# Attention, experts and a dense layer in one kernel: moving a remainder, a conversion, a subtraction, a clear and two loads

## The chip, the cores and the metric

The kernel runs on one core of one Trainium2 chip. The metric is the device time of one execution in microseconds (us). A core has a matrix engine (TensorE; PE in the profile, with PEld for its weight loads), VectorE (DVE), ScalarE (ACT), GpSimd (POOL), and a queue that issues transfers (SP). Each engine runs its own instructions in their order and waits on the others by semaphores.

## The reference

```
# attention: B=2, H=8, S=576, D=64, with a bias from a small MLP on log distances
scores = q @ k.T / 8 + bias[h, i, j]
attn   = softmax(scores);  x = attn @ v            # (2, 8, 576, 64) -> (1152, 512)

# experts: E=8, F=1024; each token goes to the expert of its highest logit
logits = x @ w_gate;  e = argmax;  g = softmax(logits)[e]
h = relu(x_e @ w1[e]);  y = h @ w2[e]              # up to 288 tokens for each expert
x = g * y  (0 for a token beyond the capacity)

# dense layer: 512 -> 2048 -> 512
h = x @ w_in;  h = max(h, 0) + alpha * min(h, 0);  out = h @ w_out
```

All data is float32; w_in and w_out come as float64 words, which the kernel turns into float32 itself.

## The kernel before

**Attention and routing** (the function course). The work is cut into units (batch, pair of heads, block of 128 queries; a unit of the last 64 queries is called small). For each unit: scores on TensorE, the bias added and the row's minimum taken on VectorE (low), the exponential on ScalarE (expo), transposes of the result (turn), products with v (values). A small unit's last 64 columns are duplicated by GpSimd into a tile named dup, which the transposes read. The bias tables are computed, stored to memory and loaded again by SP. LD[s] lists what SP issues at slot s: load_bias, load (q, k, v), load_vd (a rearranged piece of v), c1 (constants of the routing), clear (zeros written to the rows that the experts read and to the output, from a tile zr that GpSimd fills once). From slot 18 on, the routing of batch 0 runs in small steps between the units, by the list late: one entry a step, two steps a unit. first_weights finds the first expert that has tokens (four small VectorE operations) and lets SP load its first quarter of weights; first_halves, on GpSimd, splits that quarter into a high part and a remainder.

**Experts.** A product in float32 is made as three products of rounded parts: high x high, high x remainder, remainder x high. A quarter q of an expert's weights becomes w1h, w1l, w2h, w2l: the high part by a cast (ScalarE, or GpSimd for the very first), the remainder by a subtraction. job runs an expert group of up to 288 tokens in eight pieces f: layer1(f) makes 12 products (g), a relu (hh) on ScalarE and its remainder (hl) on VectorE; layer2(f-1) makes 12 more (acc). yh and yl are the group's result (to_dense).

The first group's weights are split step by step between the pieces, by the table todo: at key (f, 2) or (f, 4) the words name the steps: hIQ is the cast of w1 (I=1) or w2 (I=2) of quarter Q, lIQ its remainder, so h23 l23 are w2h and w2l of the last quarter, which pieces 6 and 7 use. turn transposes the second group's rows, ahead0 and ahead1 convert pieces 0 and 1 of the last stage's weights from float64 words (f64_convert: a scaling on ScalarE, three VectorE operations, then a cast and a subtraction), jobs3 finishes the list of groups. The order of TensorE, ScalarE and VectorE is that of the code up to the end of this group.

The second group is inside a conditional block (tc.If): the engines take the branch one by one, each when it has done what it has in front of it. Inside, the order on every engine is found by the framework's scheduler. group splits its first quarter with raw_split(0, t, early=True): the cast and the subtraction of w1 on GpSimd. Its steps carry ahead(2), ahead(3), and the rider: a third group of at most 32 tokens whose products run between those of the second, with its weight quarters in borrowed buffers (the last of four in the staging tile M.d[1]).

**The dense layer** (ffn) runs 16 pieces of fg and facc products. Its weights come through three staging tiles M.d, are converted, split, and used; the first four pieces are prepared ahead.

Of the kernel before, what the change touches and what calls it, by code (L numbers as in the profile page):

```python
# [11 lines left out]
F32 = mybir.dt.float32  # L12
# [4 lines left out]
ALU = mybir.AluOpType  # L17
# [5 lines left out]
B, H, S, D = 2, 8, 576, 64  # L23
N, DM = B * S, H * D
# [16 lines left out]
def build(tc, nc, a):  # L41
    V, A, G, T, SY = nc.vector, nc.scalar, nc.gpsimd, nc.tensor, nc.sync
    with contextlib.ExitStack() as ctx:
# [164 lines left out]

        KQV, LAST = {}, [None]

# [418 lines left out]
        def raw_split(q, t, early=False):  # L629

            w = [pair(q, [128, 1024], F32R, n) for n in ("w1h", "w1l", "w2h", "w2l")]
            for i in range(2):
                if early and i == 0:
                    G.tensor_copy(w[0], t[0])
                    G.tensor_tensor(w[1], t[0], w[0].bitcast(F32), ALU.subtract)
                else:
                    halves(w[2 * i], w[2 * i + 1], t[i])
            return w

        def row_tiles():  # L640
            return [raw.tile([128, RW], F32, tag="xr", name="xj", bufs=5)[:96, 0:DM] for _ in range(3)]

        def job_rows(ts, o):
            for r in range(3):
                rows_of.other(SY.dma_start(ts[r], xd[ds(o + 96 * r, 96), 0:DM]))

# [3 lines left out]
        def turn_rows(ts, r, t):  # L650
            for d in range(4):
                T.transpose(t[:, 96 * d:96 * d + 96], ts[r][:, 128 * d:128 * d + 128], ident[:96, :96])

# [93 lines left out]
        def rider(g, e, yo):  # L747
# [9 lines left out]

            def cell2(q):
                S[q] = (AH["more"], *g1.t)[q] if q < 3 else M.d[1].bitcast(F32)
                return S[q]  # L760

            def load1(q):
                SY.dma_start(cell2(q).rearrange("p (k c) -> p k c", k=4),
                             w1[:, 256 * q:256 * q + 256].rearrange("(k p) c -> p k c", p=128))

            def load2(q):
                SY.dma_start(cell2(q).rearrange("p (f n) -> p f n", f=2),
                             w2[256 * q:256 * q + 256, :].rearrange("(f p) n -> p f n", p=128))

# [12 lines left out]
            def partial(q):  # L782
                w = S[q].rearrange("p (k c) -> p k c", k=4)
                ps = ps1(pt, "part")[:, 0:256]
                for k in range(4):
                    T.matmul(ps[n * k:n * k + n], x[:, k], w[:, k], start=True, stop=True, skip_group_check=True)
                R.p = cell()[:, 0:256]
                A.copy(R.p, ps)
# [7 lines left out]
            def layer2(q):  # L796
                if q == 0:
                    R.acc = ps1(pt, "racc")[:, 0:256]
                w = S[q].rearrange("p (f n) -> p f n", f=2)
                for j in range(2):  # L800
                    for d in range(2):
                        o = n * (2 * j + d)
                        T.matmul(R.acc[o:o + n], R.h[:, n * (2 * q + j):][:, 0:n], w[:, j, 256 * d:256 * d + 256],
                                 start=q == 0, stop=q == 3, skip_group_check=True)
# [55 lines left out]
        def fetch_more():  # L860
            z = xp.tile([128, 2048], F32, tag="xT1", name="ah1")
            for j in range(2, PRE):
                AH[j] = z[:, 512 * j - 1024:512 * j - 512]
            AH["more"] = z[:, 1024:2048]
            f64_load(3, M.d[0])
# [123 lines left out]
        def course():  # L989
# [107 lines left out]
            for i in range(n):  # L1097
                u, t, w = [U[z] if z >= 0 else None for z in (i, i - 2, i - 3)]
                s = starts.get(id(u))
                if s is not None:  # L1100
# [138 lines left out]
        def lower(q, i):  # L1239
# [7 lines left out]
        call = dict(st, fetch=fetch_ahead, more=fetch_more, jobs1=jobs1, jobs2=lambda: first(jobs2), jobs3=jobs3,  # L1247
                    turn0=g1.todo[0][1], turn=g1.todo[1][1], **{f"ahead{i}": lambda i=i: ahead(i) for i in range(2)})
        call.update((f"{z}{i + 1}{q}", lambda q=q, i=i, f=f: f(q, i)) for q in range(4) for i in range(2)
# [20 lines left out]
        with tc.If(J.mode == 1) as course:  # L1270
            two_groups(prepare(2, 0), *[(2 * i + 1, lambda i=i: ahead(i)) for i in range(2, PRE)])
            ffn(0, 608)
        with course.Else():
            with tc.If(J.mode > 0) as course:
                group(g1, False, stepper(*[(2 * i + 1, lambda i=i: ahead(i)) for i in range(2, PRE)]))
                ffn(0, 608)
            with course.Else():
                jobs_rest()
                for i in range(2, PRE):
                    ahead(i)  # L1280
# [99 lines left out]
```

## Time and profile before

| | |
|---|---|
| Runs (device us) | 359.82, 360.06, 363.24; median 360.06 |
| The profiled execution | 363.0 us, of which 361.3 us lie between its first and last instruction |
| Granted TensorE clock, mean | 0.992 |
| Busy, share of the span | PE 94%, PEld 76%, DVE 77%, ACT 66%, POOL 17% |
| Transfers | 76.89 MB, mean 213 GB/s |

The busy shares are of the whole span, and the stages have different limits: in the attention part ScalarE and VectorE are nearly as busy as TensorE, in the dense layer TensorE is full. The clock is a share of full speed; it has two levels, 0.5 and 1. In a timeline a line gives the start, the duration, the engine, the line of the code, the operation, what it writes and reads, and in brackets the idle time before it with what ended that. A line may merge several operations (x4). In a view by stretches a line gives the stretch, its length, the busy time (with the number of instructions) of PE, PEld, DVE, ACT and POOL, the granted clock, the share of the transfer engines' time, and GB/s.

### The profile page before, as it was taken

How to read it: one execution, taken by the hardware profiler on the slowest of the kernel's cores; microseconds unless marked ns; L12 is line 12 of the kernel's file. 1: busy time of each engine (PE TensorE's matmuls, PEld its weight loads, DVE VectorE, ACT ScalarE, POOL GpSimd, SP SyncE). 2: the span in 40 equal slices, each digit the busy share in tenths (PEclk: the TensorE clock that was granted, in tenths of full speed). 3: DMA queues.
4: the chain of work that ended last, by engine and by line, in shares of the span. 5: the costliest groups of instructions: out<-in, count | busy, mean ns of one | idle time of the engine just before them, and what ended most of it. 6: DMA issues, size and time to landing. Idle time of an engine off the chain costs nothing. (4 is left out here: it accounts for less than half of the span.)

```text
span 361.3 us, 8966 instructions
## 1 busy us (share of the span) xinstructions
PE 341.3 (94%) x3372; PEld 276.1 (76%) x3373; DVE 278.4 (77%) x673; ACT 237.4 (66%) x585; POOL 61.6 (17%) x91
## 2 busy tenths in 40 slices
PE   4999999998999999999999799999999999999992
PEld 2424565566899888888899797799898898898881
DVE  5979988967788867876788975169999999988330
ACT  6959998986667666767764383348677576566430
POOL 2056333200000010670261400020000000000013
PEclk9999999999999999999999899999999999999998
DMA  7789979897999854928735894653545656430003
GB/s 298 203 261 319 343 262 358 290 306 293 407 352 254 281 190 121 368 97 256 220 96 179 296 319 131 229 175 121 191 156 178 182 166 205 145 118 3 0 14 132
DMA packets 42016, 76.89 MB, mean 213 GB/s; under 512 B 5127, under 2 KB 19591, under 8 KB 41964
## 3 DMA queue, kind: packets, MB, share of 16 engines
q1 hardware_dynamic: 40780, 73.76, 62.2%
q0 software_dynamic: 1184, 2.48, 1.9%
q8 instruction: 28, 0.46, 0.5%
q14 instruction: 24, 0.20, 0.2%
HBM read 57.53 MB, written 20.09 MB: 215 GB/s over the span
## 5 line engine op out<-in xcount | busy, mean ns | idle before, releaser
L273 ACT ACTIVATE p<-p,mn 128x576 f32<-128x576 f32 x72 | 55.6, 779 | 10.7 <-DVE mn L266 10.3
L259 PE MATMUL sps<-kqv 64*128 64x288 f32 x256 | 59.8, 425 | 0.0
L266 DVE CUSTOM_DVE_ANT_0 p<-sps,bias 128x576 f32<-128x576 f32 x72 | 52.2, 750 | 7.4 <-PE sps L252 2.7
L305 PE MATMUL t<-ident,p 64*128 64x64 f32 x640 | 52.5, 227 | 1.9 <-ACT st L200 0.8
L305 PEld LDWEIGHTS t<-ident,p 64*128 64x128 f32 x640 | 45.3, 139 | 6.6 <-ACT st L200 2.5
L183 DVE TENSOR_SCALAR h<-c 128x512 f32<-128x512 f32 (+17 forms) x121 | 49.2, 471 | 0.9 <-PE bps L192 0.8
L280 ACT COPY PT<-t 128x320 f32<-128x320 f32 (+1 forms) x85 | 30.0, 405 | 24.6 <-PE sps L259 18.5
L192 PE MATMUL bps<-h,c 128*32 128x512 f32 (+17 forms) x352 | 36.2, 504 | 6.6 <-DVE h L183 5.1
L259 PEld LDWEIGHTS sps<-kqv 64*128 64x128 f32 x256 | 36.9, 187 | 7.2 <-issue 4.0
L323 PE MATMUL av<-PT,kqv 128*64 128x128 f32 x512 | 35.3, 279 | 0.8 <-ACT pt L280 0.3
L323 PEld LDWEIGHTS av<-PT,kqv 128*64 128x64 f32 x512 | 27.5, 136 | 8.5 <-ACT PT L280 3.7
L845 ACT ACTIVATE cv<-d 128x512 f32<-128x512 f32 x32 | 21.5, 676 | 15.7 <-DMA d<-in_win 7.7
L200 ACT ACTIVATE st<-bps,c 128x527 f32<-128x527 f32 (+35 forms) x72 | 30.8, 507 | 1.0 <-PE bps L192 1.0
L940 PE MATMUL facc<-w2h,hl 128*128 128x512 f32 (+1 forms) x75 | 29.7, 396 | 0.0
L940 PE MATMUL facc<-w2h,hh 128*128 128x512 f32 (+1 forms) x75 | 29.6, 395 | 0.0
L940 PE MATMUL facc<-w2l,hh 128*128 128x512 f32 (+1 forms) x75 | 29.6, 395 | 0.0
L192 PEld LDWEIGHTS bps<-h,c 128*32 128x32 f32 x352 | 11.8, 115 | 23.1 <-DVE h L183 7.3
L179 POOL TENSOR_SCALAR h<-c 128x448 f32<-128x448 f32 (+11 forms) x12 | 21.1, 1761 | 37.0 <-PE bps L192 19.6
L928 PE MATMUL fg<-yh,w1l 128*128 128x304 f32 x120 | 26.6, 302 | 0.0
L928 PE MATMUL fg<-yl,w1h 128*128 128x304 f32 x120 | 26.5, 302 | 0.0
L928 PE MATMUL fg<-yh,w1h 128*128 128x304 f32 x120 | 26.5, 302 | 0.0
L282 DVE COPY PT<-t 128x320 f32<-128x320 f32 (+1 forms) x43 | 18.8, 461 | 8.9 <-PE t L305 8.0
(232 smaller groups left out, 698.2 us busy)
## 6 DMA issues: line engine op xcount, KB each, us to landing
bias<-bd SPq DMA_DIRECT2D x23, 576.0 KB, 6.2
bd<-st SPq DMA_DIRECT2D x36, 295.5 KB, 5.3
raw<-in_ew SPq DMA_DIRECT2D x20, 512.0 KB, 5.5
d<-in_win SPq DMA_DIRECT2D x16, 512.0 KB, 3.8
d<-in_wout SPq DMA_DIRECT2D x16, 512.0 KB, 3.9
kqv<-in_kqva SPq DMA_DIRECT2D x6, 736.0 KB, 6.3
kqv<-in_kqvb SPq DMA_DIRECT2D x6, 672.0 KB, 8.0
xd<-zr SPq DMA_DIRECT2D x4, 722.8 KB, 8.4
```

Of the source, the lines that this page charges most:

```text
L183: V.tensor_scalar(h, tab[:, :n], psi[:, i:i + 1], 0.0, ALU.add, ALU.max)
L192: T.matmul(ps[32 * c:32 * c + 32, n0:n1], w2n, hs[c][:, n0:n1], start=True, stop=True)
L200: A.activation(st[:, o:o + src.shape[1]], src, AF.Copy, scale=rr[:, t:t + 1])
L259: return [lambda n=n: T.matmul(ps[:, n, :288], q[u.ul][p], k[p, 288 * n:288 * n + 288], start=True, stop=True) for n in range(2)]
L266: V.tensor_tensor_reduce(out.rearrange("p (a b) -> p a b", a=2), ps[:, :, :288], bias.rearrange("p (a b) -> p a b", a=2), -0.125, 3.0e38, ...
L273: A.activation(out, out, AF.Exp, bias=mn, scale=-1.0, accum_out=acc)
L280: A.copy(o, i)
L305: return [lambda i=i, x=x: T.transpose(src[:, i], x[p], ident[p, p]) for i, x in enumerate(rows)], out
L323: T.matmul(o[p, c], u.v[:, j, p], rhs(h, j), start=j == 0, stop=False, skip_group_check=True)
L845: A.mul(v, r[:, :, 1].bitcast(F32), 2.0 ** -112)
L928: T.matmul(ps, w[:, 128 * k:128 * k + 128], x[:, k, s], start=k + i == 0, stop=k + i == 5)
L940: T.matmul(acc[i][:m], h[:, r:r + m], w, start=f == 0 and j == 0, stop=f == NF - 1 and j == 2)
```

## The change

Seven things change.

1. h23 l23 move in todo from (6, 2) to (5, 4).
2. ahead1 leaves todo; ahead(1) becomes a step of the second group, in front of ahead(2) and ahead(3) (steps 3, 5 and 7).
3. In raw_split with early, the subtraction that gives the first w1l goes from GpSimd to VectorE.
4. The rider's last weight quarter lies in two of the second group's spare row tiles instead of M.d[1]; each of its two loads becomes two transfers. The row tiles are now declared with all 128 partitions, of which 96 hold rows as before.
5. The two memsets of zr are placed behind the latest dup copy on GpSimd.
6. The loads of vd (batch 1) and c1 go from slots 3 and 4 to slots 7 and 8.
7. In late, first moves two steps later, to the step of s0.

```diff
             if zr is None:
                 zr = raw.tile([128, RW], F32, name="zr")
-                G.memset(zr[:, 0:DM + 1], 0.0)
-                G.memset(zr[:, DM + 1:RW], BIG)
+                behind(G.memset(zr[:, 0:DM + 1], 0.0), DUP[0])
+                behind(G.memset(zr[:, DM + 1:RW], BIG), DUP[0])
...
-                G.tensor_copy(u.dup, u.P[:, 512:576].unsqueeze(1).to_broadcast([128, 2, 64]))
+                DUP[0] = G.tensor_copy(u.dup, u.P[:, 512:576].unsqueeze(1).to_broadcast([128, 2, 64])).ins
...
                 if early and i == 0:
                     G.tensor_copy(w[0], t[0])
-                    G.tensor_tensor(w[1], t[0], w[0].bitcast(F32), ALU.subtract)
+                    V.tensor_tensor(w[1], t[0], w[0].bitcast(F32), ALU.subtract)
...
         def row_tiles():
-            return [raw.tile([128, RW], F32, tag="xr", name="xj", bufs=5)[:96, 0:DM] for _ in range(3)]
+            return [raw.tile([128, RW], F32, tag="xr", name="xj", bufs=5)[:, 0:DM] for _ in range(3)]
...
-            def cell2(q):
-                S[q] = (AH["more"], *g1.t)[q] if q < 3 else M.d[1].bitcast(F32)
-                return S[q]
+            def cells(q, n):
+
+                t = [(AH["more"], *g1.t)[q]] if q < 3 else g.ts[1:]
+                z = [z.rearrange("p (k c) -> p k c", c=n) for z in t]
+                S[q] = [x[:, j] for x in z for j in range(x.shape[1])]
+                return z
+
+            def load(q, w, n):
+                z = cells(q, n)
+                for x, y in zip(z, (w,) if len(z) == 1 else (w[:, 0:512 // n], w[:, 512 // n:])):
+                    SY.dma_start(x, y)
...
-            LD[3].append((lambda: behind(load_vd(1), LAST[0]),))
-            LD[4].append((lambda: behind(SY.dma_start(c1, a["c1"]), LAST[0]),))
+            LD[7].append((lambda: behind(load_vd(1), LAST[0]),))
+            LD[8].append((lambda: behind(SY.dma_start(c1, a["c1"]), LAST[0]),))
...
-                                  "slots first places", "r2", "s0", "r3", "s1", "r4 s2", "s3", "s4 second", "", "halves", ""):
+                                  "slots places", "r2", "first s0", "r3", "s1", "r4 s2", "s3", "s4 second", "", "halves", ""):
...
                 (2, 4): "h12 l12", (3, 2): "jobs2 turn0 h22", (3, 4): "l22", (4, 2): "ahead0 more", (4, 4): "h13 l13 jobs3",
-                (5, 4): "ahead1", (6, 2): "h23 l23", (7, 2): "turn"}
+                (5, 4): "h23 l23", (7, 2): "turn"}
...
-            two_groups(prepare(2, 0), *[(2 * i + 1, lambda i=i: ahead(i)) for i in range(2, PRE)])
+            two_groups(prepare(2, 0), *[(2 * i + 1, lambda i=i: ahead(i)) for i in range(1, PRE)])
```

The other branches of the block change in the same way (range(1, PRE) in place of range(2, PRE)), and the rider's partial and layer2 read the weights through the list S[q].

## Rows read from the trace of the kernel before

**Rows 1.** Stretches of 10 us.
```profile
200.00:210.00 10.00, 7.83 (x51) 7.42 (x51) 7.72 (x11) 4.76 (x10) 3.73 (x2) 0.83 0.85 306
210.00:220.00 10.00, 9.92 (x76) 8.90 (x76) 9.57 (x15) 7.11 (x11) 0.00 (x0) 1.00 0.67 205
220.00:230.00 10.00, 10.00 (x89) 7.45 (x92) 2.15 (x4) 3.11 (x10) 0.00 (x0) 1.00 0.78 249
```

**Rows 2.** Timeline of TensorE at the seam: start, us, what, idle before it.
```profile
202.45 0.55 PE L652 MATMUL xjT<-ident,xj 96*128 96x96 f32 x4 [0.86 <-DVE hl L685]
...
202.78 0.77 PE L696 MATMUL acc<-hh,w2h 128*128 128x288 f32 x4
...
205.39 1.33 PE L696 MATMUL acc<-hh,w2l 128*128 128x288 f32 x4 [1.31 <-DVE w2l L1240]
...
209.04 0.69 PE L681 MATMUL g<-xh,w1h 128*128 128x288 f32 x4
...
209.57 0.70 PE L681 MATMUL g<-xh,w1l 128*128 128x288 f32 x4
```

**Rows 3.** A stretch of 1 us at the seam, columns as in rows 1.
```profile
206.00:207.00 1.00, 1.00 (x7) 1.00 (x5) 1.00 (x3) 0.00 (x0) 0.00 (x0) 0.50 0.12 30
```

**Rows 4.** Timeline of all engines around the seam.
```profile
192.59 0.69 DVE L848 SCALAR_TENSOR_TENSOR cw<-cv,cw 128x512 int32<-128x512 int32 x1
...
197.78 0.45 DVE L685 SCALAR_TENSOR_TENSOR hl<-g,hh 128x288 fp32r<-128x288 f32 x1
...
200.05 0.62 ACT L602 CAST ah<-cw 128x512 fp32r<-128x512 f32 x1 [3.56 <-DVE cw L849]
...
201.56 2.69 POOL L635 TENSOR_TENSOR w1l<-raw,w1h 128x1024 fp32r<-128x1024 f32 x1
...
202.31 3.02 DVE L1240 TENSOR_TENSOR w2l<-raw,w2h 128x1024 fp32r<-128x1024 f32 x1
...
209.91 0.76 DVE L829 TENSOR_TENSOR yl<-acc,yh 128x576 fp32r<-128x576 f32 x1 [0.28 <-ACT yh L828]
...
211.06 1.23 DVE L603 TENSOR_TENSOR w2l<-raw,w2h 128x1024 fp32r<-128x1024 f32 x1 [0.40 <-ACT w2h L602]
...
213.51 1.22 DVE L603 TENSOR_TENSOR w1l<-raw,w1h 128x1024 fp32r<-128x1024 f32 x1
```

**Rows 5.** Timeline of TensorE late in the second group.
```profile
235.99 0.29 PE L696 MATMUL acc<-hh,w2h 128*128 128x288 f32 x1
```

**Rows 6.** Timelines of GpSimd, SP's queue and TensorE before the first group.
```profile
156.12 2.37 POOL L983 TENSOR_TENSOR w1l<-raw,w1h 128x1024 fp32r<-128x1024 f32 x1
...
160.24 0.97 POOL L543 DMA_INDIRECT xd<-xr,ci  x1 [0.46 <-issue]
...
162.64 1.29 SPq L645 DMA_DIRECT2D xj<-xd  x3
...
167.61 0.88 PE L652 MATMUL xjT<-ident,xj 96*128 96x96 f32 x8
```

**Rows 7.** Timeline of all engines around the clear's memsets.
```profile
85.56 0.20 ACT L273 ACTIVATION_READ_ACCUMULATOR p<-p,mn 128x1 f32 x1
...
86.94 0.53 POOL L129 MEMSET zr<- 128x513 f32 x1 [18.60 <-ACT PT L280]
...
87.79 0.27 PE L305 MATMUL t<-ident,dup 64*128 64x64 f32 x2 [1.00 <-POOL dup L276]
```

**Rows 8.** Timelines of VectorE and TensorE around the first weights' choice.
```profile
147.18 0.17 DVE L358 TENSOR_SCALAR f<-ebk 128x8 f32<-128x8 f32 x1
...
148.49 0.48 DVE L282 COPY PT<-t 128x320 f32<-128x320 f32 x1
...
149.02 0.46 PE L305 MATMUL t<-ident,p 64*128 64x64 f32 x7 [0.53 <-DVE PT L282]
```

**Rows 9.** Timelines of SP's queue and of TensorE, first half.
```profile
37.16 0.83 SPq L221 DMA_DIRECT2D vd<-in_vd  x1
...
58.19 0.27 PE L305 MATMUL t<-ident,p 64*128 64x64 f32 x1 [0.81 <-ACT st L200]
```

More of the change, by code (lines that the diff above doesn't have):

```diff
@@ L206, in bias_out @@
             SY.dma_start(dst, st[:, :nr + nf])
-        KQV, LAST = {}, [None]
+        KQV, LAST, DUP = {}, [None], [None]
         def load(b, hp, part="a"):
@@ L640, in row_tiles @@
         def row_tiles():
-            return [raw.tile([128, RW], F32, tag="xr", name="xj", bufs=5)[:96, 0:DM] for _ in range(3)]
+            return [raw.tile([128, RW], F32, tag="xr", name="xj", bufs=5)[:, 0:DM] for _ in range(3)]
         def job_rows(ts, o):
             for r in range(3):
-                rows_of.other(SY.dma_start(ts[r], xd[ds(o + 96 * r, 96), 0:DM]))
+                rows_of.other(SY.dma_start(ts[r][:96], xd[ds(o + 96 * r, 96), 0:DM]))
         def x_tiles(q=0):
@@ L651, in turn_rows @@
             for d in range(4):
-                T.transpose(t[:, 96 * d:96 * d + 96], ts[r][:, 128 * d:128 * d + 128], ident[:96, :96])
+                T.transpose(t[:, 96 * d:96 * d + 96], ts[r][:96, 128 * d:128 * d + 128], ident[:96, :96])
         def split_rows(x, r, t, few=None):
@@ L756, in cell @@
                 return M.p.tile([128, 512], F32, tag="cw", name="cell", bufs=4)
-            def cell2(q):
-                S[q] = (AH["more"], *g1.t)[q] if q < 3 else M.d[1].bitcast(F32)
-                return S[q]
+            def cells(q, n):
[7 more added lines that the diff above has]
+                    SY.dma_start(x, y)
             def load1(q):
-                SY.dma_start(cell2(q).rearrange("p (k c) -> p k c", k=4),
-                             w1[:, 256 * q:256 * q + 256].rearrange("(k p) c -> p k c", p=128))
+                load(q, w1[:, 256 * q:256 * q + 256].rearrange("(k p) c -> p k c", p=128), 256)
             def load2(q):
-                SY.dma_start(cell2(q).rearrange("p (f n) -> p f n", f=2),
-                             w2[256 * q:256 * q + 256, :].rearrange("(f p) n -> p f n", p=128))
+                load(q, w2[256 * q:256 * q + 256, :].rearrange("(f p) n -> p f n", p=128), 512)
             def begin():
@@ L782, in partial @@
             def partial(q):
-                w = S[q].rearrange("p (k c) -> p k c", k=4)
+                w = S[q]
                 ps = ps1(pt, "part")[:, 0:256]
                 for k in range(4):
-                    T.matmul(ps[n * k:n * k + n], x[:, k], w[:, k], start=True, stop=True, skip_group_check=True)
+                    T.matmul(ps[n * k:n * k + n], x[:, k], w[k], start=True, stop=True, skip_group_check=True)
                 R.p = cell()[:, 0:256]
@@ L798, in layer2 @@
                     R.acc = ps1(pt, "racc")[:, 0:256]
-                w = S[q].rearrange("p (f n) -> p f n", f=2)
+                w = S[q]
                 for j in range(2):
@@ L802, in layer2 @@
                         o = n * (2 * j + d)
-                        T.matmul(R.acc[o:o + n], R.h[:, n * (2 * q + j):][:, 0:n], w[:, j, 256 * d:256 * d + 256],
+                        T.matmul(R.acc[o:o + n], R.h[:, n * (2 * q + j):][:, 0:n], w[j][:, 256 * d:256 * d + 256],
                                  start=q == 0, stop=q == 3, skip_group_check=True)
@@ L861, in fetch_more @@
             z = xp.tile([128, 2048], F32, tag="xT1", name="ah1")
-            for j in range(2, PRE):
-                AH[j] = z[:, 512 * j - 1024:512 * j - 512]
-            AH["more"] = z[:, 1024:2048]
+            AH[2], AH[3], AH["more"] = z[:, 0:512], z[:, 512:1024], z[:, 1024:2048]
             f64_load(3, M.d[0])
@@ L1245, in build @@
                 (2, 4): "h12 l12", (3, 2): "jobs2 turn0 h22", (3, 4): "l22", (4, 2): "ahead0 more", (4, 4): "h13 l13 jobs3",
[1 row of a table removed]
+                (5, 4): "h23 l23", (7, 2): "turn"}
         call = dict(st, fetch=fetch_ahead, more=fetch_more, jobs1=jobs1, jobs2=lambda: first(jobs2), jobs3=jobs3,
-                    turn0=g1.todo[0][1], turn=g1.todo[1][1], **{f"ahead{i}": lambda i=i: ahead(i) for i in range(2)})
+                    turn0=g1.todo[0][1], turn=g1.todo[1][1], **{f"ahead{i}": lambda i=i: ahead(i) for i in range(1)})
         call.update((f"{z}{i + 1}{q}", lambda q=q, i=i, f=f: f(q, i)) for q in range(4) for i in range(2)
@@ L1274, in build @@
             with tc.If(J.mode > 0) as course:
-                group(g1, False, stepper(*[(2 * i + 1, lambda i=i: ahead(i)) for i in range(2, PRE)]))
+                group(g1, False, stepper(*[(2 * i + 1, lambda i=i: ahead(i)) for i in range(1, PRE)]))
                 ffn(0, 608)
@@ L1278, in build @@
                 jobs_rest()
-                for i in range(2, PRE):
+                for i in range(1, PRE):
                     ahead(i)
```

## The prediction

> **What bounds the kernel now.** I read the page's busy shares first: TensorE is at work for 94% of the span (the table above), so a gain has to be a wait of TensorE that goes, and any new wait of TensorE is a loss. I then read the trace in stretches of 10 us to find where TensorE is not full. From 30 to 350 us one stretch stands out: 200 to 210 us, where it is busy for 7.83 of 10 us and its granted clock averages 0.83 [rows 1]. That is the seam between the first group of experts and the second. The remaining waits were read off the timeline of TensorE, one by one; those that the change touches come below.
>
> The seam in detail. Three things add up. The last four transposes of the second group's rows wait 0.86 us for an hl, and the twelve products of piece 6 stop for 1.31 us at w2l [rows 2]. Then the clock is at half, 1.2 GHz instead of 2.4 [rows 3]. Four products of 288 columns take 0.53 us undisturbed (209.04 to 209.57 us), so the 24 from 202.78 to 209.04 us should take 3.2 us; they take 6.26, which is 3.1 lost, the 1.31 included. With the 0.86 the seam costs 3.9 us: 2.2 of waiting and 1.7 of slow clock.
>
> Why w2l is late: the remainder l23 is a subtraction on VectorE that takes 3.02 us here [rows 4], where one of the same shape takes 1.22 (213.51 us). GpSimd runs the first w1l of the next group from 201.56 to 204.25 us, almost the same time. Why hl is late: the second converted piece, ahead(1), stands in front of it. ScalarE waits 3.56 us for VectorE's conversion before it can cast, and the relu of piece 6 is behind that cast [rows 4].
>
> The Trainium skill, "GPSIMD Engine Reference", section "1. Specifications", says that GpSimd shares its SBUF interfaces with VectorE and gets in the way of VectorE instructions with two SBUF inputs. The trace agrees, 3.02 against 1.22 us. If that were the only thing that counted, taking the subtraction off GpSimd would bring back the seam's whole 3.9 us; the next part says why I do not take that.
>
> **The change part by part.**
>
> *l23 two slots earlier, ahead(1) out of piece 5.* VectorE is then free after the hl of piece 5 at 198.2 us (197.78 plus 0.45, [rows 4]); l23 takes 1.22 and is done by 199.5, before GpSimd's work starts. The hl of piece 6 follows at about 199.9 instead of just before 202.45 us, in time for the transposes, and nothing that TensorE needs in pieces 6 and 7 is late. The raw buffer that l23 frees is refilled earlier too, which only helps. Gain 3.9 us in the profiled execution; if the clock doesn't fall there in ordinary runs, 2.2.
>
> *First w1l on VectorE.* This is the price. The subtraction is inside the conditional block, and an engine runs its block only after what it has before it. The row that shows this: VectorE's first work in the block, w2l at 211.06 us, comes after the last yl of the group before (209.91 us for 0.76) [rows 4]. So w1l can start at 210.67 us in the old clock, which is 1.63 us after TensorE begins the new group (209.04), and it ends 1.22 later, at 2.85. The second set of four products of that group needs it at 0.53. GpSimd had it at 204.25 us, long before. If TensorE does nothing in between, it waits 2.85 - 0.53 = 2.3 us. The block isn't in a hand-written order, and the trace shows that a product of a step written later is put between two of an earlier one where the earlier one's operand is late: one acc product at 235.99 us, inside a g step [rows 5]. The next piece's eight products with w1h are ready, and they take 2 x 0.53 = 1.06 us. Then the wait is 1.2 us. Bounds: 0 and 2.3 us, and 4.0 if the clock falls as well (the 1.7 from above). I take 1.2, because the block shows such filling.
>
> *ahead(1) in the second group.* Its VectorE work is four operations of at most 0.69 us (one stands in [rows 4]), so up to 2.8 us, plus the w1l of 1.22. In the first 10 us of the group VectorE is already busy for 9.57, in the next 10 for 2.15 [rows 1]. So there is room, but late. What TensorE needs early is the next w1l (213.51 us, [rows 4]). Bounds for its delay beyond TensorE's own: 0, if the added conversions stand behind it, and 1.9 us, if the first w1l (1.22) and one conversion (0.69) stand in front and nothing gives way. I take 0.4, nearer to the lower end, because most of the added work can wait until 220 us and TensorE, held at the first w1l, comes later as well; that wait is the cover.
>
> *The last piece of the rider in the row tiles.* Two transfers in place of one, twice. SP's queue has two more issues of 0.43 us each (three row loads take 1.29, [rows 6]). Behind them in the queue are the loads of the last quarter and of the next stage, none of which TensorE waits for in this group. The staging buffer d1 comes free at ahead(1) instead of after the rider's last product, so the final stage's first load is earlier. No wait of TensorE stands there, so both are worth 0; if the loads are what is late next, the two issues cost 0.9, and -0.9 to 0.9 are the ends that I keep.
>
> *The clear behind the copy.* GpSimd spends 86.94 to 87.5 us on the two memsets and only then makes the copy of the remainder (dup), whose data ScalarE had ready at 85.76 (85.56 plus 0.20). TensorE waits 1.00 us for it [rows 7]. With the memsets behind the later copy, dup is done by about 86.1 and the wait is gone. The memsets feed stores that are issued several steps later, so they cost nothing at their new place. Gain 0.6 (the memsets alone) to 1.0; I take 1.0.
>
> *The first weights' choice two steps later.* Its four small VectorE operations, of 0.17 us like the first, begin at 147.18 us, and the copy of PT behind them and the slot arithmetic starts at 148.49; TensorE waits 0.53 for that [rows 8]. Moved, that wait goes, and the same four are added two steps later, where they may delay a copy in the same way. So the gain is 0 to 0.5; I take 0.4. The load of the first expert's first quarter starts one unit later on SP, some 4 us by my estimate; behind it there stand the row loads, which wait for the scatters anyway.
>
> *Constants later.* vd and c1 leave SP's queue at 37 to 40 us and come back some 20 us later. The stores of the bias tables around them move by up to 0.8 us, the issue time of vd [rows 9]. TensorE's longest wait from 30 to 80 us is 0.81 us, for ScalarE, not for a transfer. So 0, with -0.5 to 0.5.
>
> **The sum.** Against the profiled execution (363.0 us, span 361.3): 3.9 + 1.0 + 0.4 - 1.2 - 0.4 = 3.7 gained, 359.3 us. That execution is 2.9 us longer than the median of 360.06, and its slow clock of 1.7 us may be part of this, since the two quicker runs must save something somewhere. Without it the gain against the median is 2.2 + 1.0 + 0.4 - 1.2 - 0.4 = 2.0, which gives 358.1 us; with it 356.4. I take 358.1 for the median.
>
> **The rivals.**
>
> *A. The wait moves to w1l.* VectorE's w1l stands behind the yl, TensorE has nothing to fill with, and the clock falls there instead. For: 2.3 us is longer than each of the two waits that now lower the clock. Against: the filling in [rows 5]. Price 2.3 + 1.7 + 0.4 against gains of 2.2 + 1.4, so 0.8 slower than the median: 360.9 us. It decides from the point at which the new wait, with its clock, is more than the 3.6 us gained. The Trainium skill, "TensorE: Matmul & The Clock Gate", section "Part 1: The HAM clock gate (the "warmup" mystery)", has it that an engine left idle falls to 1.2 GHz; the trace agrees, 0.50 in [rows 3].
>
> *B. GpSimd's order turns against the scatters.* In the kernel before, GpSimd makes the first w1h and w1l up to 158.5 us, and the last scatter goes out at 160.24; the row loads follow at 162.64, and TensorE takes the rows at 167.61 [rows 6]. If the later load leaves the w1h and w1l in front of the last scatter, this slips by up to 4 us. From the issue of the last row load (162.64 plus 1.29) to their use are 3.7 us, in which they have to land, so the slack is between 0 and 3.7 and the wait between 0.3 and 4; I take 2. Against: GpSimd's order isn't written by hand, and with the load late the scatters are ready first. Time 358.1 + 2 = 360.1.
>
> *C. Everything is covered.* The wait at w1l is filled by other products too (the rider's transposes and partial products), and the clock had fallen in the median run. 360.06 - 3.9 - 1.4 + 0.4 = 355.2 to, without the clock, 356.9; I take 356.
>
> **How the numbers follow.** My forecast has 0.55 (its own range 356.4 to 359.5), A 0.20, B 0.10, C 0.15. The range for 8 in 10 runs from C's time to A's: 355.8 to 360.9. A measurement of this kernel can tell about 1% from no change, 356.5 to 363.7 us. C and the lower edge of the forecast lie below that: faster 0.19. Slower by over 1% needs several of the upper bounds at once, or an order in the block that I don't see: 0.04. The rest, 0.77, is within 1%.
>
> **What would show it.** In the changed profile: l23 near 1.2 us and before 200 us; no wait of TensorE at w2l; the granted clock at 1.00 in the old seam; the dup copy ahead of the zr memsets and no wait behind it; a new wait of TensorE for a w1l of the second group, of 1 to 2.3 us, right after the last yl, and eight products of the next piece in front of it if filled. Wrong would be: no such wait (C), a half clock behind it (A), row transposes that wait near 167 us (B), or VectorE late with the next w1l by more than 1 us.

## The result, and the profile after

The changed kernel takes 363.09 us (median of 20 executions, 360.61 to 366.24) against 360.48 us for the kernel before on the same chip (358.1 to 365.81). The ratio is 1.0074, with a 95% interval of 1.0050 to 1.0098: some 2.7 us slower, less than 1%. The forecast was 358.1 us with a range up to 360.9, so it was wrong by 5 us and in its sign; 0.4 us of this lie in the kernel before, which takes 360.48 us here and 360.06 where the forecast started. The profiled execution is at 365.01 us, its span 363.3, the granted clock 0.989 on average. The profiled executions of two experiments below (e2 and e7) were longer than those kernels' ordinary ones; their rows are read for single waits, not for the total.

The first view is again that of 10 us stretches: length, busy time (instructions) of PE, PEld, DVE, ACT, POOL, granted clock, transfer share, GB/s. These are the lines that answer to [rows 1]:

```profile
200.00:210.00 10.00, 7.82 (x59) 7.59 (x59) 7.41 (x12) 6.32 (x11) 1.04 (x1) 0.94 1.07 360
210.00:220.00 10.00, 10.00 (x73) 9.22 (x71) 8.42 (x13) 5.32 (x10) 0.00 (x0) 0.89 0.45 139
```

The seam was repaired and TensorE is exactly as little busy as before, 7.82 of 10 us against 7.83, and in the next stretch the clock is now below 1. The timelines of TensorE and VectorE say what took the place of the old waits. They answer to [rows 2, 4].

```profile
200.09 1.16 PE L652 MATMUL xjT<-ident,xj 96*128 96x96 f32 x12
...
204.28 0.82 PE L681 MATMUL g<-xh,w1h 128*128 128x288 f32 x5
207.28 0.79 PE L681 MATMUL g<-xh,w1l 128*128 128x288 f32 x4 [2.18 <-DVE w1l L635]
...
208.88 1.16 PE L681 MATMUL g<-xl,w1h 128*128 128x288 f32 x4
...
197.48 1.22 DVE L1244 TENSOR_TENSOR w2l<-raw,w2h 128x1024 fp32r<-128x1024 f32 x1
...
202.09 1.01 DVE L603 TENSOR_TENSOR xl<-xjT,xh 128x384 fp32r<-128x384 f32 x2
204.35 1.55 DVE L835 TENSOR_TENSOR yl<-acc,yh 128x576 fp32r<-128x576 f32 x2 [1.24 <-ACT yh L834]
205.99 1.23 DVE L635 TENSOR_TENSOR w1l<-raw,w1h 128x1024 fp32r<-128x1024 f32 x1
```

Read from the top. The twelve transposes run without a wait, where four of them waited 0.86 us [rows 2]. l23 takes 1.22 us and is over before 199 us, where it took 3.02 [rows 4]. The second group begins at 204.28, 4.19 us after the first transpose; in [rows 2] it began at 209.04. So far every step came as forecast. Then TensorE stops for 2.18 us at w1l. VectorE makes it at 205.99, right behind the last yl, in front of which it stood idle for 1.24 us. Only one product of the next piece fills the gap ("x5" in place of x4), not eight. Four products that take 0.53 us at full clock are 0.96 us apart from 208.88 on, and a stretch of 1 us there shows why:

```profile
210.00:211.00 1.00, 1.00 (x6) 1.00 (x5) 1.00 (x2) 0.03 (x1) 0.00 (x0) 0.50 1.08 333
```

The granted clock is 0.50, the lower of the two levels (1.2 GHz), as it was at the old seam [rows 3]; TensorE had been idle for 2.18 us and back at work for about 1.5 when it fell. By the two rows of 10 us above, the fall costs 1.7 us (10 x 0.06 and 10 x 0.11). That is rival A, place and mechanism.

The early part, which answers to [rows 7, 8]:

```profile
82.94 0.29 POOL L276 COPY dup<-p 128x128 f32<-128x128 f32 x1 [14.80 <-ACT p L273]
91.15 0.29 POOL L276 COPY dup<-p 128x128 f32<-128x128 f32 x1 [7.92 <-ACT p L273]
91.56 0.53 POOL L129 MEMSET zr<- 128x513 f32 x1
...
153.36 1.09 PE L323 MATMUL av<-PT,kqv 128*64 128x128 f32 x16 [1.65 <-issue]
```

The dup copy no longer stands behind the memsets, and no wait of TensorE stands at it. The wait of 0.53 us at 149 us [rows 8] is gone too, but TensorE now loses 1.65 us at 153 us, two steps later, where the choice of the first expert was put. The row names no engine that ended it ("issue"), so its cause isn't shown. In the last stage this execution lost 2.4 us more between 319 and 332 us, after a transfer that came late:

```profile
264.29 0.66 ACT L851 ACTIVATE cv<-d 128x512 f32<-128x512 f32 x1 [2.58 <-DMA d<-in_wout]
...
325.78 0.55 PE L932 MATMUL fg<-yh,w1h 128*128 128x304 f32 x2 [0.59 <-ACT g L935]
```

### The profile page after: what moved, and what is told of

It reads as the page before. It is cut to its first block, busy times and chain, and to the rows that moved or that the text cites. A ratio compares the mean times of both kernels' runs of the same rounds, so it can differ in the third digit from the quotient of the medians.

```text
span 363.3 us, 8967 instructions
## 1 busy us (share of the span) xinstructions
PE 342.3 (94%) x3372; PEld 275.6 (76%) x3373; DVE 277.6 (76%) x674; ACT 236.8 (65%) x585; POOL 60.6 (17%) x90
## 5 line engine op out<-in xcount | busy, mean ns | idle before, releaser
L259 PE MATMUL sps<-kqv 64*128 64x288 f32 x256 | 60.7, 426 | 0.2 <-DVE mn L266 0.2
L192 PE MATMUL bps<-h,c 128*32 128x512 f32 (+17 forms) x352 | 35.2, 503 | 7.5 <-DVE h L183 5.5
L179 POOL TENSOR_SCALAR h<-c 128x448 f32<-128x448 f32 (+11 forms) x12 | 22.4, 1866 | 36.2 <-PE bps L192 18.5
```

Of the source, the lines that this page charges most:

```text
L179: G.tensor_scalar(h, tab[:, :n], psi[:, i:i + 1], 0.0, ALU.add, ALU.max)
L192: T.matmul(ps[32 * c:32 * c + 32, n0:n1], w2n, hs[c][:, n0:n1], start=True, stop=True)
L259: return [lambda n=n: T.matmul(ps[:, n, :288], q[u.ul][p], k[p, 288 * n:288 * n + 288], start=True, stop=True) for n in range(2)]
```

## The experiments

The theories. W: the loss is the first w1l on VectorE, because of its place behind the last yl, with the slow clock behind the wait. R: VectorE has too much to do in the second group, whatever the order. L: the last stage has become slower for a lasting reason. E: an early edit costs. Later, for the seam, V (its old waits vary from one execution to the next) against C (they are always there). S is the prediction's own term for the later choice of the expert. All ratios are to the kernel before on the same chip, with 95% intervals.

**e1: w1l back on GpSimd, all else changed.**

```diff
-                    V.tensor_tensor(w[1], t[0], w[0].bitcast(F32), ALU.subtract)
+                    G.tensor_tensor(w[1], t[0], w[0].bitcast(F32), ALU.subtract)
```

> The changed kernel with one thing undone: the first w1l goes back to GpSimd. Theory W (the wait for w1l on VectorE, 2.2 us, and the half clock behind it, 1.6, are what makes the change slow): both are gone, l23 stays near 1.2 us, the second group starts at about 204 us without a wait, and the time is 1 to 2.5 us under the kernel before, 0.993 to 0.997. Theory L (the last stage is bound by VectorE's chain of conversions, so that what TensorE gains at the seam is given back there as waits for hl and g, and more VectorE work in the second group makes it worse): the wait for w1l goes, but TensorE waits 1 to 4 us in the last stage, and the time is 0.998 to 1.006 of before.

Measured: 357.38 us, ratio 0.9943 (0.9922 to 0.9964), faster than both kernels. GpSimd has the quarter early, and TensorE takes it without a wait:

```profile
199.06 2.40 POOL L635 TENSOR_TENSOR w1l<-raw,w1h 128x1024 fp32r<-128x1024 f32 x1
...
203.19 0.70 PE L681 MATMUL g<-xh,w1l 128*128 128x288 f32 x4
```

The last stage takes 109.48 us from its first product to the start of its last, as in the kernel before, and L had 0.998 or more. One line of the change is worth more than the whole loss.

**e2: the seam alone.** l23, ahead(1) and the rider's last quarter are as changed; w1l is on GpSimd, and the clear, the constants and the first choice are as before.

```diff
-                (5, 4): "ahead1", (6, 2): "h23 l23", (7, 2): "turn"}
+                (5, 4): "h23 l23", (7, 2): "turn"}
```

> The kernel before with only the moves at the seam: l23 two slots earlier, ahead(1) in the second group, the rider's last quarter in row tiles; w1l on GpSimd, the clear, the constants and the first weights' choice as before. Theory W: the seam's 2.2 us of waiting and up to 1.7 of slow clock go, nothing takes their place: 0.991 to 0.996. Theory L: the seam's waits go, the last stage takes back what TensorE gained: 0.998 to 1.005. Theory E (one of the early edits is what costs): like W, since no early edit is in it.

Measured: 359.46 us, ratio 1.0009 (0.9980 to 1.0038). From the first row transpose to the second group it takes 4.19 us, no wait in it, and still nothing is gained, where W had 0.991 to 0.996. That was the second surprise. The time lies in L's range, but the last stage takes its 109.48 us here too, so L's mechanism isn't there. The profile also shows what the clear can cost when it stays where it was:

```profile
88.88 0.53 POOL L129 MEMSET zr<- 128x513 f32 x1 [21.26 <-DMA kqv<-in_kqvb]
...
89.72 0.37 PE L305 MATMUL t<-ident,dup 64*128 64x64 f32 x2 [3.28 <-POOL dup L276]
```

The memsets wait for a load here, and the copy behind them waits too: 3.28 us of TensorE, where [rows 7] had 1.00.

**e3: the early part alone** (clear, constants, first choice; seam and w1l as before).

```diff
-            LD[3].append((lambda: behind(load_vd(1), LAST[0]),))
+            LD[7].append((lambda: behind(load_vd(1), LAST[0]),))
...
-                                  "slots first places", "r2", "s0", "r3", "s1", "r4 s2", "s3", "s4 second", "", "halves", ""):
+                                  "slots places", "r2", "first s0", "r3", "s1", "r4 s2", "s3", "s4 second", "", "halves", ""):
```

> The kernel before with only the three early edits: the clear behind the copy, the constants later, the first weights' choice two steps later. Theory W: the wait of 1.0 us at dup and that of 0.5 at PT go, some of it comes back as a wait near 153 us: 0.996 to 0.999. Theory L: the earlier start of all later stages carries VectorE with it, so the same 0.996 to 0.999. Theory E: a new wait of 1.7 us or more near 153 us, or a later start: 1.002 to 1.007.

Measured: 359.73 us, ratio 0.9986 (0.9957 to 1.0015), 0.5 us against 1.4 in the prediction; E, which had 1.002 or more, falls. Its seam, which is that of the kernel before, waits 0.72 and 1.32 us, but at full clock. These rows are used below:

```profile
198.31 1.04 POOL L634 CAST w1h<-raw 128x1024 fp32r<-128x1024 f32 x1 [9.30 <-DMA raw<-in_ew]
199.44 2.70 POOL L635 TENSOR_TENSOR w1l<-raw,w1h 128x1024 fp32r<-128x1024 f32 x1
...
198.71 1.18 DVE L603 TENSOR_TENSOR ah<-cw,ah 128x512 fp32r<-128x512 f32 x1 [0.69 <-ACT ah L602]
...
200.19 3.03 DVE L1240 TENSOR_TENSOR w2l<-raw,w2h 128x1024 fp32r<-128x1024 f32 x1
```

**e4: w1l on VectorE alone**, in the kernel before.

```diff
-                    G.tensor_tensor(w[1], t[0], w[0].bitcast(F32), ALU.subtract)
+                    V.tensor_tensor(w[1], t[0], w[0].bitcast(F32), ALU.subtract)
```

> The kernel before with only the first w1l on VectorE. l23 isn't slowed by GpSimd any more, so it takes 1.2 us instead of 3.0 and the wait at w2l is gone or under 0.3 us; the wait of 0.86 us for hl at the transposes stays; a wait of 2 to 2.4 us for w1l comes at the start of the second group. Theory W: with the clock at half after it, 1.000 to 1.006. Theory L: the last stage's VectorE chain is 1.2 us longer at its start; 1.002 to 1.008.

Measured: 362.88 us (six executions), ratio 1.0109 (1.0069 to 1.0148), the highest ratio of all and above what either theory had. The wait is there by itself, behind the yl again, and one product stands in front of it again. The clock stays at 1.00 behind it in this profile.

```profile
206.86 0.90 PE L681 MATMUL g<-xh,w1h 128*128 128x288 f32 x5
209.77 0.81 PE L681 MATMUL g<-xh,w1l 128*128 128x288 f32 x4 [2.01 <-DVE w1l L635]
...
206.85 1.55 DVE L829 TENSOR_TENSOR yl<-acc,yh 128x576 fp32r<-128x576 f32 x2
208.49 1.23 DVE L635 TENSOR_TENSOR w1l<-raw,w1h 128x1024 fp32r<-128x1024 f32 x1
```

Together e1 and e4 show which edit loses the time. They don't show why: place (W) or load (R).

**e5: w1l still on VectorE, but in front of the last yl.** GpSimd makes a second cast of the same quarter for it, and w1l lies in the space that ahead(1) fills later.

```diff
+        def w1l_first():
+            t, s = g1.t[0], AH["more"].bitcast(F32R)
+            g1.l = AH["z"][:, 2:4].rearrange("p a b -> p (a b)")
+            G.tensor_copy(s, t)
+            V.tensor_tensor(g1.l, t, s.bitcast(F32), ALU.subtract)
...
-                (5, 4): "h23 l23", (7, 2): "turn"}
+                (5, 4): "h23 l23", (7, 2): "turn w1l_first"}
```

> The changed kernel, but the first w1l of the second group is subtracted on VectorE in the hand-written order behind the row transposes of piece 7, in front of the two last yl (GpSimd makes a second cast of the same quarter for it, and w1l lies in the space of ahead(1)). VectorE still does the subtraction, 1.22 us. W (the cost is the place behind the last yl): VectorE stood idle for 1.24 us in front of that yl, so the subtraction fits there, TensorE's wait of 2.18 us at w1l is gone, the clock stays full behind it, and the time falls by 3.8 to 4.7 us against the changed kernel, to 357 to 358 us, ratio to the kernel before 0.992 to 0.997. R (VectorE has too much to do in the second group, whatever the order): the same work stays in the same 20 us, at most the wait of 2.18 us moves to the next w1l, and the ratio stays at 1.003 or more.

Measured: 358.15 us, ratio 0.9980 (0.9955 to 1.0006), a little short of W's 0.992 to 0.997. On the same chip the changed kernel (e7, below) has 1.0067, so the place is worth 2.8 us (360.98 against 358.15), the added cast included. VectorE does the same subtraction in the gap in front of the yl:

```profile
200.61 1.01 DVE L603 TENSOR_TENSOR xl<-xjT,xh 128x384 fp32r<-128x384 f32 x2
201.54 1.22 DVE L1252 TENSOR_TENSOR ah<-raw,ah 128x1024 fp32r<-128x1024 f32 x1
202.87 1.55 DVE L836 TENSOR_TENSOR yl<-acc,yh 128x576 fp32r<-128x576 f32 x2
...
203.32 0.69 PE L682 MATMUL g<-xh,ah 128*128 128x288 f32 x4
```

The yl starts 0.08 us after the second group, exactly as in e1, and TensorE doesn't wait. R falls: the engine and its load are the same, only the order differs (e10, below, takes load away and keeps the order).

**e6: w1l needed four products later.**

```diff
-                if f == 0:
+                if f == 0 and given:
                     terms = [terms[i] for i in (0, 2, 1)]
```

> The changed kernel, with the terms of the first piece of the second and third group in the order w1h xh, w1h xl, w1l xh, so that w1l is needed after eight products and not after four. W: the wait at w1l is 2.18 less the 0.53 us of four products, 1.65 us; if the clock still falls behind it the time is 0.5 us less than the changed kernel, 362.5; if 1.65 us is too short to bring the clock down, 2 us less, 361. R: no change of the time, 363.

Measured: 360.79 us, ratio 1.0054 (1.0019 to 1.0089). The wait shrinks as W has it, though a little less, and the clock stays at 1.00 behind it. The time is 0.2 us below e7's, less than the intervals can tell, so by the time alone R's "no change" fits as well. In this profile the last stage loses 2.1 us, as in the profile after.

```profile
205.38 0.81 PE L681 MATMUL g<-xh,w1l 128*128 128x288 f32 x4 [1.78 <-DVE w1l L635]
```

**e7: the changed kernel again.** No edit.

> The changed kernel once more, for a second profile. If the wait of 2.18 us at w1l, the half clock behind it and the 2.4 us lost late in the last stage belong to the kernel, all three stand here again and the ratio to the kernel before is 1.0074 as measured. If the half clock and the late loss belong to one execution, only the wait stands here, with the last stage at 109.5 us and the second group at some 38 us.

Measured: 360.98 us, ratio 1.0067 (1.0038 to 1.0097). All three losses stand in this second profile, the wait with the same 2.18 us, 0.50 for the clock at 210 to 212 us, and the late transfer. The clock falls once more, behind waits of 0.89 and 0.27 us at the first group's row transposes:

```profile
207.70 0.79 PE L681 MATMUL g<-xh,w1l 128*128 128x288 f32 x4 [2.18 <-DVE w1l L635]
...
264.78 0.66 ACT L851 ACTIVATE cv<-d 128x512 f32<-128x512 f32 x1 [2.58 <-DMA d<-in_wout]
...
168.00:171.00 3.00, 3.00 (x34) 2.17 (x34) 0.78 (x3) 0.67 (x4) 0.00 (x0) 0.50 0.94 331
```

**e10: ahead(1) back in the first group at (6, 2), w1l still on VectorE.**

```diff
-                (5, 4): "h23 l23", (7, 2): "turn"}
+                (5, 4): "h23 l23", (6, 2): "ahead1", (7, 2): "turn"}
```

> The changed kernel with ahead1 put back into the hand-written order at (6, 2), the first w1l still on VectorE and l23 still at (5, 4). W: the wait at w1l stays between 2.0 and 2.3 us, since it comes from the place behind the last yl, and the time stays at 362 to 364 us. R: without the 2.8 us of ahead(1) in the second group VectorE has room, the second group takes 36 us, and the time falls to 359 to 360 us.

Measured: 361.07 us, ratio 1.0072 (1.0040 to 1.0105), no better than the changed kernel. VectorE comes later to the second group, so part of the wait is now one line earlier, at xl, and the rest at w1l; the seam is 1.05 us longer than the repaired 4.19 and the wait is 1.47, together 2.5 against 2.18. R had 359 to 360.

```profile
204.28 0.89 PE L681 MATMUL g<-xh,w1h 128*128 128x288 f32 x5 [0.64 <-DVE xl L603]
206.64 0.80 PE L681 MATMUL g<-xh,w1l 128*128 128x288 f32 x4 [1.47 <-DVE w1l L635]
```

The filler is one product here too, with a wait of 1.47 as with 2.18 or 2.01 (in e6, with its other order, there is none). The order of TensorE in the built kernel holds just that product at that place, whatever happens in the execution.

**e8: e1 without the later constants and the later choice** (so seam, clear, and w1l on GpSimd; the constants are back at slots 3 and 4).

```diff
-                                  "slots places", "r2", "first s0", "r3", "s1", "r4 s2", "s3", "s4 second", "", "halves", ""):
+                                  "slots first places", "r2", "s0", "r3", "s1", "r4 s2", "s3", "s4 second", "", "halves", ""):
```

> The seam with w1l on GpSimd and the clear, without the later constants and without the later choice of the first expert. W: those two are worth nothing or cost a little (the waits at 150 to 156 us that came with the later choice are 1.1 us in the profile against 0.5 us that went at 148.5), so the time is that of the version with all but w1l, or 0.5 us less: ratio to the kernel before 0.991 to 0.996, and the wait of 0.53 us at 149 us stands again. S (the prediction's own term for the later choice): 0.4 us more than that version.

**e12: e1 again, on the chip of e8.** No edit to e1.

> The changed kernel with w1l back on GpSimd once more, beside its parts on one chip. If the first measurement holds, ratio 0.994; by the version with w1l in front of the yl, which has the same waits in its profile, 0.998. The sum of the parts' profile terms (seam 2.2 to 3.9, clear 0.9, second group and first choice -0.9) says 2.2 us without the half clock, 0.994.

Measured: e8 357.91 us, ratio 0.9956 (0.9928 to 0.9985); e12 358.00 us, 0.9969 (0.9941 to 0.9997). The old wait is back in e8, and it doesn't make it slower:

```profile
148.33 0.46 PE L305 MATMUL t<-ident,p 64*128 64x64 f32 x7 [0.53 <-DVE PT L282]
```

In its place e12 waits further on, at the first group's row transposes:

```profile
165.24 1.13 PE L652 MATMUL xjT<-ident,xj 96*128 96x96 f32 x8 [0.69 <-DMA xj<-xd]
```

So the later choice and constants bring nothing that can be measured. Both versions are faster than both kernels.

**e11: the clear alone**, in the kernel before.

```diff
-                G.memset(zr[:, 0:DM + 1], 0.0)
-                G.memset(zr[:, DM + 1:RW], BIG)
+                behind(G.memset(zr[:, 0:DM + 1], 0.0), DUP[0])
+                behind(G.memset(zr[:, DM + 1:RW], BIG), DUP[0])
```

> The kernel before with the clear's memsets behind the dup copy, and nothing else. W: the wait of 1.00 us at the dup copy is gone, 0.6 to 1.0 us less, ratio 0.997 to 0.9985. Rival: the memsets' delay holds the stores of the clear or the wait moves to another copy, ratio 1.000 or more.

Measured: 358.43 us, ratio 0.9983 (0.9952 to 1.0013): 0.6 us, with zero inside the interval. No wait stands at the dup copy.

**e13: the seam alone again.** No edit to e2.

> The seam part alone with w1l on GpSimd once more, for an undisturbed profile. W: no wait at the seam, some 0.7 us given back in the second group, so 1.5 to 2 us less than the kernel before, ratio 0.994 to 0.996, and a dup wait of 1 us. Rival: the seam's waits were hidden in most executions and the part is worth nothing, as the first measurement said, ratio 1.000.

Measured: 358.74 us, ratio 0.9996 (0.9967 to 1.0025). Nothing again, with a clean seam of 4.19 us. So what it replaces can't usually have cost 2 us.

**e14, e15, e16: the kernel before, three more profiles.** One execution each, beside one of 360.67 us.

> The kernel before once more, for its profile. Theory V (the seam's collision depends on which engine starts its subtraction first, and that varies): in some executions w2l starts before GpSimd's w1l and takes under 1.6 us, and from the row transposes to the second group it is 5.0 us; in others GpSimd is first, w2l takes 3.0 us and it is 6.8 to 8.3 us. Theory C (constant collision): 6.8 to 8.3 us each time, and the seam part must then lose 2 us elsewhere.

> As the run before it: V gives 5.0 us in some of the three, C 6.8 to 8.3 us in all.

> As the two runs before it: V gives 5.0 us in some of the three, C 6.8 to 8.3 us in all.

Measured: 357.58, 358.88 and 360.05 us. From the first transpose to the second group they take 4.98, 4.98 and 5.00 us, against 8.28 in the profile of [rows 2], where the first transpose starts at 200.76 us:

```profile
200.76 0.82 PE L652 MATMUL xjT<-ident,xj 96*128 96x96 f32 x8
```

In all three TensorE waits only at the transposes, 0.23 to 0.25 us, not at w2l, and the clock stays at 1.00. These are rows of e14:

```profile
198.25 0.82 PE L652 MATMUL xjT<-ident,xj 96*128 96x96 f32 x8
...
199.31 0.55 PE L652 MATMUL xjT<-ident,xj 96*128 96x96 f32 x4 [0.23 <-DVE hl L685]
...
203.23 0.77 PE L681 MATMUL g<-xh,w1h 128*128 128x288 f32 x4
...
198.19 0.69 DVE L603 TENSOR_TENSOR ah<-cw,ah 128x512 fp32r<-128x512 f32 x1 [0.69 <-ACT ah L602]
...
199.43 1.43 DVE L1240 TENSOR_TENSOR w2l<-raw,w2h 128x1024 fp32r<-128x1024 f32 x1 [0.18 <-ACT w2h L1237]
...
198.24 1.54 POOL L634 CAST w1h<-raw 128x1024 fp32r<-128x1024 f32 x1 [8.81 <-ACT ah L602]
199.86 3.26 POOL L635 TENSOR_TENSOR w1l<-raw,w1h 128x1024 fp32r<-128x1024 f32 x1
```

Put them beside the rows of e3. There GpSimd's cast starts 0.40 us in front of VectorE's ah (198.31 against 198.71); ah takes 1.18 us, w2l comes 0.75 us after GpSimd's subtraction and takes 3.03. Here the cast starts 0.05 us behind ah; ah takes 0.69, w2l is 0.43 us ahead of GpSimd's subtraction and takes 1.43, and it is GpSimd's that takes longer. A shift of less than half a microsecond turns the collision round. The other profiles in which both engines subtract there agree: in e11 (4.98 us), e15 and e16 the cast starts 0.05 to 0.41 us behind ah and w2l takes 1.43; in the profile that the prediction read it starts 0.26 us in front of ah and w2l takes 3.02. So the long form stands in two of six. (e4, where GpSimd doesn't subtract, has 5.06 us.) V holds, C falls.

**e17: the changed kernel, third profile.** One execution.

> The changed kernel, third profile. The wait at w1l is 2.18 us again, whatever the rest. If the half clock belongs to that wait, some 3 us at half clock follow it. If the late loss of the last stage belongs to the kernel, the last stage takes 111 to 112.5 us, if not 109.5 us.

Measured: 358.49 us. The wait is 2.18 us once more. The half clock isn't there, and the last stage takes 109.47 us.

```profile
204.82 0.80 PE L681 MATMUL g<-xh,w1l 128*128 128x288 f32 x4 [2.18 <-DVE w1l L635]
...
200.00:210.00 10.00, 7.82 (x60) 7.59 (x59) 8.18 (x13) 7.14 (x11) 0.00 (x0) 1.00 1.08 356
210.00:220.00 10.00, 10.00 (x85) 8.03 (x84) 7.72 (x12) 4.47 (x10) 0.00 (x0) 1.00 0.50 169
```

So the wait belongs to the kernel, and the fall of the clock doesn't come in each execution. How often it comes can be read without a profile: each execution has a span and a mean granted clock, and span x (1 - clock) is the time lost to the slow level. In all profiles 1.0 to 2.5 us of it lie after TensorE's last product, where the clock falls too and costs nothing. This is a row of e12, whose last product starts at 348.29:

```profile
352.00:356.00 4.00, 0.00 (x0) 0.00 (x0) 0.00 (x0) 0.00 (x0) 0.00 (x0) 0.50 0.11 33
```

With the 1.7 us of a fall on the way, wherever it lies, that makes 2.7 us or more. So much is lost in 17 of 19 executions of the changed kernel in the first comparison and 8 of 12 in e7, in 4 of 6 in e4, in 5 of 11 and 4 of 12 in e6 and e10, whose waits are shorter or split; but in 10 of 91 of the kernel before (three sets of runs), 3 of 12 in e5, none of 24 in e1 and e8. The medians are 3.3 us (first comparison) and 2.9 (e7) against 1.8 for the kernel before (in each of the three sets) and 1.6 for e5. So most executions of the changed kernel pay for the clock on top of the wait, 1.1 to 1.5 us by the medians, e17 being one that didn't.

## Why the prediction was wrong, step by step

*First w1l on VectorE: the step that failed first.* The prediction found the place (behind the last yl), the wait without filling (2.3 us, measured 2.18 in three profiles) and the clock as an upper bound (4.0). It then took 1.2, "because the block shows such filling". [rows 5] shows one product put between, and one product is what came (e4, e7, e10, e17); the eight were an extrapolation. The price was 2.8 us on one chip (e7 against e5) and 3.9 us in e4 (1.09% of 359.8); 2.0 to 2.2 of waiting and 1.1 to 1.5 of clock, 3.1 to 3.7 together, lie between the two. An upper bound that needs no new mechanism, only that the scheduler doesn't help, should have been the value.

*The seam: right in mechanism, mis-sized by the execution.* Every row came as described: l23 at 1.22 us, no wait at w2l, none at the transposes. But the gain of 2.2 to 3.9 us was priced from a profile whose seam was 3.3 us longer than the usual one. Against the usual 4.98 the seam gains 0.8 us. The prediction saw that its profile was 2.9 us over the median and gave 1.7 of it to the clock; it left the 2.2 of waiting in, which was mostly the same accident. The hl in front of the transposes was part of it: the prediction put that wait (0.86 us) down to ahead(1), but with ah at 0.69 us it is 0.23 (e14), and 0.72 where ah met GpSimd's cast and took 1.18 (e3).

*The rider in the row tiles: taken at 0, costs 0.56 us.* This was read in the traces, not tried alone. Ahead of the yT products, e13 has the two halves of the last quarter apart:

```profile
229.67 0.63 PE L809 MATMUL racc<-xj,cell 128*32 128x256 f32 x4
...
230.69 0.62 PE L809 MATMUL racc<-xj,cell 128*32 128x256 f32 x4
```

and e14 has them together:

```profile
231.04 0.64 PE L803 MATMUL racc<-d,cell 128*32 128x256 f32 x8
```

Eight in one run take the 0.57 us to the next product (231.61), and four alone take 0.56 (230.23). Two transfers made two runs, so it is twice 0.56; the profile after and e17 have the same two runs, 0.55 to 0.56 us each. It is most of the 0.7 us by which the second group is longer in e13 than in e14 (35.91 against 35.21 us from its first product to the last stage), and with it the seam part's 0.8 is spent: e2 and e13 measure nothing.

*ahead(1) in the second group.* Taken at 0.4; no wait of TensorE for it was seen, and e10, which undoes it, isn't faster. The term was too high, and small.

*The clear.* Right in mechanism, 1.0 forecast, 0.6 measured with zero in the interval (e11). The wait that it removes varies as well: 1.00 in [rows 7], 3.28 in e2, 0.61 in e4, 0.87 in e13, 1.53 in e16, none listed in e14 and e15. In e16 the clock fell behind it as well:

```profile
88.00:90.00 2.00, 2.00 (x14) 1.08 (x12) 0.73 (x3) 1.05 (x4) 0.00 (x0) 0.50 1.03 389
```


*The first choice later.* 0.4 forecast, and nothing in e8 against e12, whose intervals of about 1 us either way couldn't tell 0.4 from 0. The wait of 0.53 us went, but all nine profiles with the later choice lose something after it: at 150 to 156 us (1.65 us in the profile after), or at the row transposes near 165 us (0.36 to 1.16 us in e5, e6, e7, e10, e12, e17). The nine profiles without it show no wait at those transposes. *The constants:* 0, as forecast.

*The rivals.* A came true, its clock in most executions: wait and clock were priced at 4.0 and measure 3.1 to 3.7. Its time of 360.9 missed because the gains that it was set against were too large (3.6, of which seam and clear gave 1.4), because the rider's 0.56 was in no sum, and by the 0.4 us of the kernel before. B came in small: GpSimd has w1h and w1l in front of the last scatter, waits 1.0 to 1.7 us for their load in e5, e6, e7, e10, e12 and e17, and the rows are late by the 0.36 to 1.16 us just named (in e7 with a fall of the clock behind it), where 2 was the price. It is part of why the early gains are missing, not of the loss: e1, e5 and e12 carry the same edit. C didn't come.

*The sum from ordinary executions.* Seam -0.8, second group +2.75 (37.95 in e17 against 35.2 us: 2.18 of waiting and 0.56 of the rider), clock +1.1 to 1.5, clear -0.6: +2.5 to 2.9 us. Measured are 2.7 (0.74%) and 2.4 us (0.67%). Without w1l and the clock the same sizes, with the rider's 0.56, give -0.8 us, a ratio of 0.998, for e1, e8 and e12; the intervals of e8 and e12 allow it, while e1 is half a microsecond or more better than that, for which no cause was found.

*Left open.* The late transfer of the last stage stands in the changed kernel's first two profiles and, with 1.62 us, in e6, and the last stage is 2.1 to 3.1 us longer in these three; in e17 the transfer's wait is 0.79, in the others at most 0.66. I have no cause for it. It came in three of the six profiles with a wait at w1l and in none of the twelve without, so whether the change favours it is open, and the sum leaves it out. In e7's ordinary executions there is little room for it: their span x clock is 1.3 us above that of the kernel before, and seam, second group and clear make up 1.35. Nor do the profiles tie the clock's fall to a length of the wait: the same 2.18 us brought it down twice and once not, 2.01 (e4) did not, 1.53 at the dup copy (e16) and 0.89 with 0.27 at the rows (e7) did. Only over many executions does it come more often with the longer wait.

## What to carry to other kernels

A wait that is read in one execution may be an accident of that execution; a wait that follows from the order of the instructions is there each time. Take a second profile before pricing what a change removes, and price what it adds from the order, without help from a scheduler that you haven't seen give it. When work moves to another engine, look first at what that engine has in front of it at that point; the same subtraction one place earlier in VectorE's queue cost nothing that could be measured (e5).

## What was not expected of the hardware

Two subtractions of the same shape that meet on GpSimd and VectorE don't share the cost. The one that starts first keeps nearly its own time and the other pays: VectorE 3.03 us behind GpSimd's 2.70 in e3, but 1.43 against GpSimd's 3.26 in e14, where alone they take 1.22 and, with little beside it, 2.40 us (e1). As an estimate, the second ends as if it had waited for the first: in e3 GpSimd's ends at 202.14, and 1.22 us more give 203.36, where VectorE's ends at 203.22; in e14 VectorE's ends at 200.86, and 2.40 more give 203.26, where GpSimd's ends at 203.12. That the start decides was read in six profiles and not tried alone. And four of the rider's products with 32 output rows take as long as eight, 0.56 against 0.57 us, so a run of them shouldn't be split.
